# First batch of a two-part kernel: first cast ahead of the inducing points, denominators from the summed exps, idle products in the waits

## The chip, the cores and the metric

The kernel runs on one core of a Trainium2 chip. The metric is device microseconds of that core for one execution. Every execution also lists its span (first to last instruction in the profiler's clock) and the mean granted clock of TensorE over it.

## The reference

```
def mab(q, kv):                       # scale = 1/sqrt(128)
    a = softmax(scale * q @ kv.T);  return a @ kv
h   = mab(I, x)                       # I: 32 inducing points, x: 4 x 12416 x 128
y   = mab(x, h).reshape(49664, 128)
g, v = y @ w_gate, y @ w_val          # 128 x 1536 each
out = y + sigmoid(y @ w_res) * ((gelu(g) * v) @ w_out)
```

A batch has 12416 tokens, 97 blocks of 128, loaded as 13 tiles of up to 8 blocks. h of a batch must be complete before the second attention of that batch can start. For batches 2 to 4 that is done behind the work of the batch before; for the first batch nothing is there to hide it. The change edits only this start.

## The kernel before

PE multiplies, ACT takes exps and gelus and copies, DVE multiplies gelu by value and casts, POOL adds and casts. The loading of the first batch, with cuts marked:

```
wb = bank_f()
for i in range(WARM):                          # 9 products on zeros, ahead of all else
    pe.matmul(wb, warm[:, :P], warm[:, :TOK], start=True, stop=True)
i1t_ps = bank_g()
pe.transpose(i1t_ps[:, :M], ind_f, ident[:M, :M])     # inducing points
ve.tensor_copy(I1T, i1t_ps[:, :M])
...
convert_hi(0, 0, ve)                           # cast of tile 0
for n in range(ntile + 2):
    if n + 1 < ntile:
        convert_hi(0, n + 1, act if n == 0 else ve)
    if n < ntile:
        turn_pe(0, n, act if n < 10 and n % 2 == 0 or n == ntile - 1 else ve)
    if 1 <= n <= ntile:
        exps("a", 0, n0, n0 + w, bank_v())     # n0, w of tile n - 1
        if n < ntile - 1:
            add_up(n0, w)                      # POOL: s += e
        if n == ntile - 1:
            weight_cast(2, act)
    if n >= 2:
        ...                                    # total(): column sums of s and the last e into acc
        accumulate(0, n0, n0 + w, n == 2, n == ntile + 1)     # sums of h, tile n - 2
```

`total` put the denominators of the softmax into a 129th column of the accumulator (ones as moving operand, s as stationary one). After the last sum all 129 columns were copied (nacc in the profile); `turn_first_h` turned the denominators by one more product, inverted them (zi) and scaled the turned h (ht):

```
pe.matmul(tp[:, 0:M], na[:, P:P + 1].to_broadcast([P, P]), strips[:, 0, :], ...)
pe.matmul(tp[:, P:2 * P], na[:, 0:P], row, ...)
ve.reciprocal(zi, tp[:, 0:M])
ve.tensor_tensor(ht, tp[:, P:2 * P], zi, AL.mult)             # shapes cut
```

Then come the exps of the second attention, the first layer with h folded into the weights, a table load on ACT and the first gelus. From there a fixed order of products, gelus and multiplications runs to the end.

The softmax here doesn't subtract the row's maximum and nothing guards it: scores larger than these inputs give would overflow.

Of the kernel before, what the change touches and what calls it, by code (L numbers as in the profile page):

```python
# [9 lines left out]
FP32 = mybir.dt.float32  # L10
# [4 lines left out]
AL = mybir.AluOpType  # L15
# [3 lines left out]
def kernel(  # L19
# [25 lines left out]
    P = 128  # L45
# [3 lines left out]
    FCH = F // P  # L49
    nblk = N // P  # L50
    PRE = 8
    WARM = 9
    ntile = (nblk + PRE - 1) // PRE
    Q = 4
    scale = 1.0 / math.sqrt(C)
# [26 lines left out]
    def bank_g():  # L82
        return ps_g.tile([P, TOK], FP32, name="g", tag="g")

    def bank_v():
        return ps_v.tile([P, 2 * TOK], FP32, name="v", tag="v")

    def bank_f():
        return ps_f.tile([P, TOK], FP32, name="f", tag="f")
# [4 lines left out]
    def blocks_of(k):  # L94
        return k * PRE, min(PRE, nblk - k * PRE)
# [20 lines left out]
    def convert_hi(b, k, eng):  # L116
        _, w = blocks_of(k)
        hi_t[b, k] = hi = sized(p_hl, w, P, "hi")
        if eng is act:
            act.activation(hi[:, :w, :], xf_t[b, k][:, :w, :], AC.Copy, bias=0.0, scale=1.0)  # L120
        else:
            eng.tensor_copy(hi[:, :w, :], xf_t[b, k][:, :w, :])  # L122
# [15 lines left out]
    def turn_pe(b, k, eng=act):  # L138
        _, w = blocks_of(k)
        xt = sized(p_xt, w, P, "xt")  # L140
        xt_t[b, k] = xt
        tps = bank_g().bitcast(FP16).rearrange("p (k c) -> p k c", c=P)
        for j in range(w):
            pe.transpose(tps[:, j, :], hi_t[b, k][:, j, :], identF)  # L144
        if eng is act:
            act.activation(xt[:, :w, :], tps[:, :w, :], AC.Copy, bias=0.0, scale=1.0)
        else:
            eng.tensor_copy(xt[:, :w, :], tps[:, :w, :])
# [28 lines left out]
    def accumulate(b, j0, j1, first, last):  # L177
        if first:
            acc_t[b] = bank_f() if b == 0 else bank_g()
        acc = acc_t[b]  # L180
        for j in range(j0, j1):
            k, jj = divmod(j, PRE)
            cq = j % Q
            o = acc[cq * M:(cq + 1) * M, :]
            e = e_of.pop(("a", b, j))
            if b == 0:
                pe.matmul(o[:, 0:P], e, xf_t[b, k][:, jj, :],  # L187
                          start=(first and j < j0 + Q), stop=(last and j + Q >= j1),
                          skip_group_check=True)
                continue  # L190
            pe.matmul(o[:, 0:P + 1], e, lo_t[b, k][:, jj, :P + 1],
                      start=(first and j < j0 + Q), stop=False, skip_group_check=True)
            pe.matmul(o[:, 0:P], e, hi_t[b, k][:, jj, :],
                      start=False, stop=(last and j + Q >= j1), skip_group_check=True)
        if last:
            if b not in nacc_t:
                nacc_t[b] = p_h.tile([P, P + 1], FP32, name="nacc", tag="nacc", bufs=1)
                ve.tensor_copy(nacc_t[b], acc[:, :P + 1])
            else:
                na = nacc_t[b]  # L200
                ve.tensor_tensor(na, acc[:, :P + 1], na, AL.add)
            del acc_t[b]

    def add_up(n0, w):

        e = e_t["a", n0 // WIDE * WIDE][:, n0 % WIDE * M:(n0 % WIDE + w) * M]
        if "s" not in e_of:
            e_of["s"] = p_sm.tile([P, PRE * Q * M], FP16, name="a2", tag="a2").bitcast(FP32)[:, :w * M]
            po.tensor_copy(e_of["s"], e)
        else:  # L210
            po.tensor_tensor(e_of["s"], e_of["s"], e, AL.add)

    def total(s):

        n = s.shape[1]
        for q in range(0, n, Q * M):
            r = min(Q * M, n - q)
            pe.matmul(acc_t[0][:r, P:P + 1], s[:, q:q + r], one,
                      start=False, stop=False, skip_group_check=True)

    def finish_h(b, hs=None):
        if hs is None:
            hs = bank_g()
            pe.matmul(hs[:, 0:P + 1], strips.rearrange("p q m -> p (q m)"), nacc_t.pop(b),
                      start=True, stop=True)
        rz = p_h.tile([P, 1], FP32, name="rz1", tag="rz1")
        ve.reciprocal(rz, hs[:, P:P + 1])
        hf = p_h.tile([P, P + 1], FP32, name="nacc", tag="nacc", bufs=1)[:, :P]
        ve.tensor_scalar(hf, hs[:, 0:P], rz, None, op0=AL.mult)
        hf_t[b] = hf  # L230

        hra = p_h.tile([P, 2, P], FP16, name="hra", tag="hra")
        hra_t[b] = hra
        po.memset(hra[2 * M:, 0, :], 0.0)
        po.memset(hra[:2 * M, 1, :], 0.0)
        po.tensor_copy(hra[2 * M:, 1, :], hf[2 * M:, :])
        po.tensor_tensor(hra[3 * M:, 1, :], hf[3 * M:, :], hra[3 * M:, 1, :], AL.subtract)

        if b not in hgv_t:
            hgv_t[b] = p_h.tile([P, F], BF16, name="hgv", tag="hgv")  # L240

    def turn_first_h(b):

        na = nacc_t[b]
        tp = bank_g()
        row = strips.rearrange("p q m -> p (q m)")
        pe.matmul(tp[:, 0:M], na[:, P:P + 1].to_broadcast([P, P]), strips[:, 0, :],
                  start=True, stop=True)
        pe.matmul(tp[:, P:2 * P], na[:, 0:P], row, start=True, stop=True)
        zi = p_h.tile([P, M], FP32, name="zi", tag="zi", bufs=1)  # L250
        ve.reciprocal(zi, tp[:, 0:M])
        ht = p_h.tile([P, P], FP16, name="ht", tag="ht")
        ve.tensor_tensor(ht.rearrange("p (q m) -> p q m", m=M),
                         tp[:, P:2 * P].rearrange("p (q m) -> p q m", m=M),
                         zi.unsqueeze(1).to_broadcast([P, Q, M]), AL.mult)
        ht_t[b] = ht
        hgv_t[b] = p_h.tile([P, F], BF16, name="hgv", tag="hgv")
# [12 lines left out]
    def first_layer_out(b, c, bank):  # L270
        ve.tensor_scalar(hgv_t[b][:, c:c + TOK], bank, parts, None, op0=AL.mult)
# [243 lines left out]
    ve.tensor_tensor(strips[:, 0, :], strips[:, 0, :], ident[:, 3 * M:4 * M], AL.add)  # L515
    for q in range(1, Q):
        ve.tensor_copy(strips[:, q, :], strips[:, 0, :])
    wb = bank_f()
    for i in range(WARM):
        pe.matmul(wb, warm[:, :P], warm[:, :TOK], start=True, stop=True)  # L520
    i1t_ps = bank_g()
    pe.transpose(i1t_ps[:, :M], ind_f, ident[:M, :M])
    ve.tensor_copy(I1T, i1t_ps[:, :M])

    pieces = []
    for dst, src, o, w in ((wG, moe_w_gate, 0, TOK), (wV, moe_w_val, 0, TOK),
                           (wG, moe_w_gate, TOK, 2 * TOK), (wV, moe_w_val, TOK, 2 * TOK),
# [15 lines left out]
    def weight_cast(i, eng):  # L543
        dst, src, w = pieces[i]
        if eng is act:
            act.activation(dst, staged.pop(i)[:, :w], AC.Copy, bias=0.0, scale=1.0)
        else:
            eng.tensor_copy(dst, staged.pop(i)[:, :w])
# [2 lines left out]
    for i in range(len(pieces)):  # L551
        weight_in(i)

    tiles = list(range(ntile))
    convert_hi(0, 0, ve)
    for n in range(ntile + 2):
        if n + 1 < ntile:
            convert_hi(0, n + 1, act if n == 0 else ve)
        if n < ntile:
            turn_pe(0, n, act if n < 10 and n % 2 == 0 or n == ntile - 1 else ve)  # L560
        if 1 <= n <= ntile:
            n0, w = blocks_of(n - 1)
            exps("a", 0, n0, n0 + w, bank_v())
            if n < ntile - 1:
                add_up(n0, w)
            if n == ntile - 1:
                weight_cast(2, act)
        if n >= 2:
            n0, w = blocks_of(n - 2)
            if n == ntile:  # L570
                total(e_of.pop("s"))
                total(e_t["a", n0 // WIDE * WIDE][:, n0 % WIDE * M:(n0 % WIDE + w) * M])
            if n == ntile + 1:
                total(e_t["a", n0 // WIDE * WIDE][:, :w * M])
            accumulate(0, n0, n0 + w, n == 2, n == ntile + 1)
    weight_cast(0, po)
    weight_cast(1, po)
    weight_cast(3, act)
    weight_cast(4, po)
    turn_first_h(0)  # L580
    half = PRE // 2
    exps("b", 0, 0, half, bank_g())
    sums_b(0, 0, half, ve)
# [4 lines left out]
    sums_b(0, half, WIDE, po)  # L588
    layers = bank_v()
    first_layer(0, 0, layers[:, :TOK])  # L590
    first_layer(0, TOK, layers[:, TOK:])
    first_layer_out(0, 0, layers[:, :TOK])
    exps("b", 0, WIDE, 2 * WIDE, bank_v())
    turned()
    later = [(j0, min(j0 + WIDE // 2, nblk)) for j0 in range(2 * WIDE, nblk, WIDE // 2)]
    for j in later:
        exps("b", 0, *j, bank_g())
    first_layer_out(0, TOK, layers[:, TOK:])
    weight_cast(5, po)
    ones_b(0, half, WIDE)  # L600
# [8 lines left out]
    def rest_of_first():  # L609
        layers = bank_v()  # L610
        first_layer(0, 2 * TOK, layers[:, :TOK])
        rs, hs = layers[:, TOK:TOK + P], layers[:, TOK + P:TOK + 2 * P + 1]
        pe.matmul(rs[:64, :], ht_t[0][:, :64], wR, start=True, stop=True)
        pe.matmul(hs, strips.rearrange("p q m -> p (q m)"), nacc_t.pop(0), start=True, stop=True)
        first_layer_out(0, 2 * TOK, layers[:, :TOK])
        finish_h(0, hs)
        res_layer(0, ve, rs)
# [249 lines left out]
```

## Time and profile before

| view of the kernel before | value |
|---|---|
| time of the first three runs, median | 773.27 us (772.80 to 773.37) |
| profiled execution | 771.35 us, span 769.6, clock 0.989 |
| busy PE, ACT, DVE | 97%, 97%, 96% of the span |
| half clock within the first 50 us | 3.41 + 3.41 + 10.23 us |
| first product on DVE | 37.23 us |

How to read it: with three engines at 96 to 97% over 769.6 us, what is left to win is where the digits of the clock row and of the first slices are below 9. The lines themselves are shown in the prediction.

### The profile page before, as it was taken

Reading aid. Unit: us, or ns where it says so; the run is one execution under the profiler, and the core shown is the slowest. Engines: PE = TensorE matmul, PEld = TensorE weight load, DVE = VectorE, ACT = ScalarE, POOL = GpSimd, SP = SyncE. Lnnn points to the kernel's source line nnn. Section 1 sums busy time; section 2 is a strip of 40 time slices with the busy share of each in tenths; the row PEclk is TensorE's granted clock in tenths of the full one; section 3 lists DMA queues with packets and bytes.
Section 4 is the critical chain, followed back from the end, with each engine's and each line's share of the span. In section 5 each row is a group of like instructions: output and inputs, shape, how many; then the busy total and the mean of one; then the engine's idle time right before and its main releaser. Section 6 shows DMA issues by size and latency. Waiting matters only on the chain.

```text
span 769.6 us, 23941 instructions
## 1 busy us (share of the span) xinstructions
PE 744.0 (97%) x9602; PEld 433.1 (56%) x9602; DVE 736.1 (96%) x737; ACT 744.0 (97%) x1494; POOL 470.4 (61%) x464
## 2 busy tenths in 40 slices
PE   8899999999999999999999999999999999999997
PEld 5545456565655555565655555566565545555654
DVE  5599999999999999989999999999999999999997
ACT  4699999999999999999999999999999999999997
POOL 3636998711777979723377788852267664543444
PEclk9889999999999999999999999999999999999999
DMA  9314598601164487510044567850006341101111
GB/s 344 124 43 121 142 214 181 150 29 43 43 114 103 119 202 199 152 42 29 30 90 101 113 164 171 201 117 30 34 25 130 73 99 43 43 29 43 42 43 47
DMA packets 118449, 78.16 MB, mean 102 GB/s; under 512 B 96672, under 2 KB 99392, under 8 KB 118336
## 3 DMA queue, kind: packets, MB, share of 16 engines
q1 hardware_dynamic: 118336, 76.62, 39.5%
q8 instruction: 75, 1.23, 0.7%
q14 instruction: 38, 0.31, 0.1%
HBM read 27.87 MB, written 25.43 MB: 69 GB/s over the span
## 4 chain that ended last, share of the span: by engine, by line
PE 48%; ACT 34%; issue 10%; DVE 5%; POOL 2%; DMA 1%; DVEq 0%; SPq 0%; ACTq 0%; POOLq 0%
ACT ge L419 25%; PE f L442 21%; PE g L408 11%; PE v L408 7%; DVE u L413 5%; PE g L450 3%; ACT th L456 3%; ACT at L461 3%; ACT fe L470 1%; ACT e L172 1%; PE g L169 1%; PE f L187 1%; PE g L144 1%; DVE th L474 1%; POOL lo L128 1%
## 5 line engine op out<-in xcount | busy, mean ns | idle before, releaser
L413 DVE TENSOR_TENSOR u<-ge,v 128x1024 bf16<-128x1024 f32 x584 | 670.8, 1212 | 6.2 <-PE v L408 1.2
L419 ACT ACTIVATE ge<-g 128x512 f32<-128x512 f32 x1164 | 605.2, 658 | 2.9 <-PE g L408 2.6
L442 PEld LDWEIGHTS <-u 128*128 128x128 bf16 x4656 | 270.3, 98 | 214.3 <-issue 209.7
L442 PE MATMUL f<-wO,u 128*128 128x128 bf16 x4656 | 374.2, 221 | 4.2 <-DVE th L474 0.9
L408 PE MATMUL g<-rt,hgv 32*128 32x512 f16 x1152 | 336.9, 381 | 7.8 <-ACT ge L419 0.5
L408 PE MATMUL v<-rt,hgv 32*128 32x512 f16 x1152 | 222.7, 386 | 1.9 <-DVE u L413 1.3
L475 POOL TENSOR_TENSOR at<-at,th 128x512 f32<-128x512 f32 (+1 forms) x99 | 123.7, 1250 | 131.4 <-ACT ge L419 40.0
L408 PEld LDWEIGHTS <-hgv 32*128 32x128 bf16 x2400 | 74.3, 91 | 87.7 <-issue 21.7
L471 POOL TENSOR_TENSOR th<-th,fe 128x512 f32<-128x512 f32 (+1 forms) x33 | 39.7, 1202 | 96.3 <-ACT fe L470 96.3
L343 POOL TENSOR_TENSOR a<-e,z 128x1024 f16<-128x1024 f32 (+1 forms) x48 | 89.8, 1880 | 8.7 <-DMA rt<-a 4.7
L128 POOL TENSOR_TENSOR lo<-xf,hi 128x1024 f16<-128x1024 f32 x36 | 76.9, 2137 | 0.2
L450 PE MATMUL g<-hra,rt 128*128 128x128 f16 x768 | 71.3, 219 | 1.3
L461 ACT ACTIVATE at<-g 128x512 f32<-128x512 f32 (+1 forms) x100 | 63.7, 647 | 0.1
L456 ACT ACTIVATE th<-g 128x512 f32<-128x512 f32 (+1 forms) x100 | 63.4, 646 | 0.2
L450 PEld LDWEIGHTS <-rt 128*128 128x128 f16 x768 | 50.6, 97 | 9.6 <-issue 7.7
L474 DVE SCALAR_TENSOR_TENSOR th<-th,f 128x512 f32<-128x512 f32 (+1 forms) x67 | 45.4, 678 | 3.3 <-PE f L442 1.5
L122 POOL CAST hi<-xf 128x1024 f16<-128x1024 f32 x36 | 37.3, 1037 | 14.4 <-DMA xf<-in_x_dram 12.4
L472 POOL TENSOR_TENSOR at<-at,fe 128x512 f32<-128x512 f32 (+1 forms) x33 | 39.7, 1203 | 0.0
L319 POOL TENSOR_TENSOR a<-e 128x512 f32<-128x512 f32 (+1 forms) x12 | 15.3, 1278 | 22.4 <-ACT e L172 22.4
L169 PEld LDWEIGHTS <-xt 128*128 128x128 f16 x768 | 23.7, 97 | 5.0 <-issue 3.8
L172 ACT ACTIVATE e<-g 128x512 f32<-128x512 f32 (+3 forms) x40 | 20.9, 602 | 2.3 <-PE g L169 2.3
L322 POOL TENSOR_TENSOR a<-a 128x256 f32<-128x256 f32 (+8 forms) x48 | 20.1, 418 | 3.8
(136 smaller groups left out, 259.7 us busy)
## 6 DMA issues: line engine op xcount, KB each, us to landing
out_dram<-at SPq DMA_DIRECT2D x96, 256.0 KB, 2.3
xf<-in_x_dram SPq DMA_DIRECT2D x39, 512.0 KB, 4.4
ge<-in_x_dram SPq DMA_DIRECT2D x9, 512.0 KB, 7.6
rt<-a SPq DMA_TRANSPOSE x48, 3.1
xt<-hi SPq DMA_TRANSPOSE x36, 4.3
ge<-in_moe_w_gate_dram SPq DMA_DIRECT2D x1, 512.0 KB, 8.3
ge<-in_moe_w_val_dram SPq DMA_DIRECT2D x1, 512.0 KB, 7.9
ge<-in_moe_w_out_dram SPq DMA_DIRECT2D x1, 512.0 KB, 7.3
```

Source lines behind the costliest of these rows:

```text
L128: eng.tensor_tensor(lo[:, :w, :P], xf_t.pop((b, k))[:, :w, :], hi_t[b, k][:, :w, :], AL.subtract)
L343: eng.tensor_tensor(a2[:, :n], ev[:, o:o + n, :].unsqueeze(2).to_broadcast([P, n, Q, M]), z[:, o:o + n].unsqueeze(2).unsqueeze(3).to_broad ...
L408: pe.matmul(*t[n], start=True, stop=True)
L413: ve.tensor_tensor(u[:, :n], ge_t.pop(value)[:, :n], v_t.pop(value)[:, :n], AL.mult)
L419: act.activation(ge_t[i][:, h * TOK:h * TOK + n], gb[:, :n], AC.Gelu, bias=0.0, scale=1.0)
L442: pe.matmul(self.ffn[:, k, :], u_t[self.gi, si][:, o:o + P], wO[:, fc, :], start=first, stop=not self.todo, skip_group_check=True)
L450: pe.matmul(bank[:, k * P:(k + 1) * P], rt_t[self.b, self.k][:, self.j0 + k, :], hra_t[self.b][:, s, :], start=True, stop=True)
L456: act.activation(self.th[:, :self.tw], self.mix(0), AC.Tanh, bias=0.0, scale=0.5)
L461: act.activation(self.at[:, :self.tw], self.mix(1), AC.Copy, bias=0.0, scale=1.0)
L471: po.tensor_tensor(th, th, fe, AL.mult)
L474: ve.scalar_tensor_tensor(th, th, 1.0, f, AL.add, AL.mult)
L475: (ve if self.gi == ngrp - 1 else po).tensor_tensor(at, at, th, AL.add)
```

## The change

The intent is to bring the first products forward and to keep TensorE's clock up meanwhile. An idle product is a product on zeros whose result is never read; it only keeps PE busy. Core of the diff (helpers cut):

```diff
-        ve.tensor_copy(nacc_t[b], acc[:, :P + 1])
+        n = P + (b > 0)
+        ve.tensor_copy(nacc_t[b][:, :n], acc[:, :n])
-    def total(s):                       # column sums into acc[:, P:P + 1]
+    def total(zb):
+        s = e_of.pop("s")
+        for k in (ntile - 2, ntile - 1):
+            ...
+            ve.tensor_tensor(s[:, :w * M], s[:, :w * M], e, AL.add)
+        n = s.shape[1] // M
+        for j in range(n):
+            pe.matmul(zb, one.to_broadcast([P, P]), s[:, j * M:(j + 1) * M],
+                      start=(j == 0), stop=(j == n - 1))
+    def idle(n, bank=None):
+        ...                             # n products 128x512 on zeros, never read
-    i1t_ps = bank_g()                   # moved behind the first turned tile
...
     convert_hi(0, 0, ve)
-    for n in range(ntile + 2):
...
+    for n in range(ntile - 1):
+        convert_hi(0, n + 1, ve)
+        turn_pe(0, n, act if n < 10 and n % 2 == 0 else ve)
+        if n == 0:
+            ...                         # inducing points
+            idle(2)
+        if n == ntile - 2:
+            turn_pe(0, n + 1, act)
+        if n >= 1:
+            step_e(n - 1)
+        if n == 1:
+            idle(2)
+        if n >= 2:
+            step_s(n - 2)
+    weight_cast(2, act)
+    step_e(ntile - 2)
+    step_e(ntile - 1)
+    step_s(ntile - 3)
+    zb = bank_g()[:, :M]
+    step_s(ntile - 2)
+    total(zb)
+    step_s(ntile - 1)
+    idle(1, bank_g())
...
-    turn_first_h(0)
+    turn_first_h(0, zb)                 # reciprocal straight from zb
+    idle(3)
...
     first_layer(0, 0, layers[:, :TOK])
-    first_layer(0, TOK, layers[:, TOK:])
...                                      # all other exps of the second attention
+    first_layer(0, TOK, layers[:, TOK:])
     first_layer_out(0, TOK, layers[:, TOK:])
...
-        pe.matmul(hs, strips..., nacc_t.pop(0), start=True, stop=True)
+        pe.matmul(hs[:, :P], strips..., nacc_t.pop(0)[:, :P], start=True, stop=True)
+        zi = e_of.pop("zi")
+        for q in range(Q):
+            pe.matmul(hs[q * M:(q + 1) * M, P:P + 1], zi, ident[:, 0:1], ...)
+        idle(5)
```

More of the change, by code (lines that the diff above doesn't have):

```diff
@@ L51 @@
     PRE = 8
-    WARM = 9
     ntile = (nblk + PRE - 1) // PRE
@@ L211, in add_up @@
             po.tensor_tensor(e_of["s"], e_of["s"], e, AL.add)
-    def total(s):
-        n = s.shape[1]
-        for q in range(0, n, Q * M):
-            r = min(Q * M, n - q)
-            pe.matmul(acc_t[0][:r, P:P + 1], s[:, q:q + r], one,
-                      start=False, stop=False, skip_group_check=True)
+    def total(zb):
+        s = e_of.pop("s")
+        for k in (ntile - 2, ntile - 1):
+            n0, w = blocks_of(k)
+            e = e_t["a", n0 // WIDE * WIDE][:, n0 % WIDE * M:(n0 % WIDE + w) * M]
+            ve.tensor_tensor(s[:, :w * M], s[:, :w * M], e, AL.add)
[4 more added lines that the diff above has]
+    def idle(n, bank=None):
+        bank = bank_f() if bank is None else bank
+        for i in range(n):
+            pe.matmul(bank, warm[:, :P], warm[:, :TOK], start=True, stop=True)
     def finish_h(b, hs=None):
@@ L226, in finish_h @@
         rz = p_h.tile([P, 1], FP32, name="rz1", tag="rz1")
-        ve.reciprocal(rz, hs[:, P:P + 1])
+        if b == 0:
+            ve.tensor_copy(rz, hs[:, P:P + 1])
+        else:
+            ve.reciprocal(rz, hs[:, P:P + 1])
         hf = p_h.tile([P, P + 1], FP32, name="nacc", tag="nacc", bufs=1)[:, :P]
@@ L240, in finish_h, with turn_first_h @@
             hgv_t[b] = p_h.tile([P, F], BF16, name="hgv", tag="hgv")
-    def turn_first_h(b):
+    def turn_first_h(b, zb):
         na = nacc_t[b]
-        tp = bank_g()
-        row = strips.rearrange("p q m -> p (q m)")
-        pe.matmul(tp[:, 0:M], na[:, P:P + 1].to_broadcast([P, P]), strips[:, 0, :],
-                  start=True, stop=True)
-        pe.matmul(tp[:, P:2 * P], na[:, 0:P], row, start=True, stop=True)
-        zi = p_h.tile([P, M], FP32, name="zi", tag="zi", bufs=1)
-        ve.reciprocal(zi, tp[:, 0:M])
+        tp = bank_g()[:, :P]
+        pe.matmul(tp, na[:, 0:P], strips.rearrange("p q m -> p (q m)"), start=True, stop=True)
+        zi = e_of["zi"] = p_h.tile([P, M], FP32, name="zi", tag="zi", bufs=1)
+        ve.reciprocal(zi, zb)
         ht = p_h.tile([P, P], FP16, name="ht", tag="ht")
         ve.tensor_tensor(ht.rearrange("p (q m) -> p q m", m=M),
-                         tp[:, P:2 * P].rearrange("p (q m) -> p q m", m=M),
+                         tp.rearrange("p (q m) -> p q m", m=M),
                          zi.unsqueeze(1).to_broadcast([P, Q, M]), AL.mult)
@@ L517 @@
         ve.tensor_copy(strips[:, q, :], strips[:, 0, :])
-    wb = bank_f()
-    for i in range(WARM):
-        pe.matmul(wb, warm[:, :P], warm[:, :TOK], start=True, stop=True)
-    i1t_ps = bank_g()
-    pe.transpose(i1t_ps[:, :M], ind_f, ident[:M, :M])
-    ve.tensor_copy(I1T, i1t_ps[:, :M])
+    idle(9)
     pieces = []
@@ L552, with step_e, step_s @@
         weight_in(i)
-    tiles = list(range(ntile))
-    convert_hi(0, 0, ve)
-    for n in range(ntile + 2):
-        if n + 1 < ntile:
-            convert_hi(0, n + 1, act if n == 0 else ve)
-        if n < ntile:
-            turn_pe(0, n, act if n < 10 and n % 2 == 0 or n == ntile - 1 else ve)
-        if 1 <= n <= ntile:
-            n0, w = blocks_of(n - 1)
-            exps("a", 0, n0, n0 + w, bank_v())
-            if n < ntile - 1:
-                add_up(n0, w)
-            if n == ntile - 1:
-                weight_cast(2, act)
-        if n >= 2:
-            n0, w = blocks_of(n - 2)
-            if n == ntile:
-                total(e_of.pop("s"))
-                total(e_t["a", n0 // WIDE * WIDE][:, n0 % WIDE * M:(n0 % WIDE + w) * M])
-            if n == ntile + 1:
-                total(e_t["a", n0 // WIDE * WIDE][:, :w * M])
-            accumulate(0, n0, n0 + w, n == 2, n == ntile + 1)
+    def step_e(n):
+        n0, w = blocks_of(n)
+        exps("a", 0, n0, n0 + w, bank_v())
+        if n < ntile - 2:
+            add_up(n0, w)
+    def step_s(n):
+        n0, w = blocks_of(n)
+        accumulate(0, n0, n0 + w, n == 0, n == ntile - 1)
+    convert_hi(0, 0, ve)
+    for n in range(ntile - 1):
+        convert_hi(0, n + 1, ve)
+        turn_pe(0, n, act if n < 10 and n % 2 == 0 else ve)
+        if n == 0:
+            i1t_ps = bank_g()
+            pe.transpose(i1t_ps[:, :M], ind_f, ident[:M, :M])
+            ve.tensor_copy(I1T, i1t_ps[:, :M])
+            idle(2)
[5 more added lines that the diff above has]
+            idle(2)
+        if n >= 2:
+            step_s(n - 2)
[8 more added lines that the diff above has]
+    idle(1, bank_g())
     weight_cast(0, po)
@@ L613, in rest_of_first @@
         pe.matmul(rs[:64, :], ht_t[0][:, :64], wR, start=True, stop=True)
-        pe.matmul(hs, strips.rearrange("p q m -> p (q m)"), nacc_t.pop(0), start=True, stop=True)
+        pe.matmul(hs[:, :P], strips.rearrange("p q m -> p (q m)"), nacc_t.pop(0)[:, :P],
+                  start=True, stop=True)
+        zi = e_of.pop("zi")
+        for q in range(Q):
+            pe.matmul(hs[q * M:(q + 1) * M, P:P + 1], zi, ident[:, 0:1], start=True, stop=True)
+        idle(5)
         first_layer_out(0, 2 * TOK, layers[:, :TOK])
```

## The prediction

> **What bounds the kernel now.** I read the page first. Its busy line has three engines at 96 to 97% of a 769.6 us span:
>
> ```profile
> PE 744.0 (97%) x9602; PEld 433.1 (56%) x9602; DVE 736.1 (96%) x737; ACT 744.0 (97%) x1494; POOL 470.4 (61%) x464
> ...
> PEclk9889999999999999999999999999999999999999
> ```
>
> The reader should see that nothing is left in the middle, and that the TensorE clock is below full only in slices 2 and 3 (19 to 58 us). The change edits only the first batch's start, which ends there. So everything turns on when the steady stream of gelu (ACT), product (DVE) and matmul (PE) begins, and at what clock. A microsecond won there moves the end by about a microsecond, because the order of instructions after it is fixed and full.
>
> Next I read the busy times in windows whose edges are the steps of the clock (columns: stretch, length, then busy of PE, PEld, DVE, ACT, POOL, then clock, DMA share, GB/s):
>
> ```profile
> 5.12:8.54 3.42, 1.38 (x18) 1.03 (x17) 1.25 (x3) 1.74 (x2) 0.00 (x0) 1.00 0.91 341
> 8.54:11.95 3.41, 3.02 (x46) 2.57 (x47) 2.23 (x4) 2.02 (x4) 0.80 (x2) 0.50 1.03 419
> 11.95:22.19 10.24, 10.24 (x252) 8.37 (x250) 8.06 (x12) 5.81 (x11) 7.36 (x8) 1.00 1.03 402
> 22.19:25.60 3.41, 2.87 (x69) 2.06 (x61) 1.08 (x3) 1.38 (x5) 2.80 (x5) 1.00 1.03 290
> 25.60:29.02 3.42, 2.29 (x31) 1.84 (x31) 0.94 (x3) 1.57 (x3) 0.30 (x1) 1.00 0.09 21
> 29.02:32.43 3.41, 3.38 (x78) 2.53 (x78) 1.91 (x4) 1.59 (x4) 1.51 (x2) 0.50 0.02 5
> 32.43:35.85 3.42, 2.81 (x44) 1.55 (x41) 1.78 (x4) 3.39 (x7) 3.19 (x7) 1.00 0.00 0
> 35.85:46.08 10.23, 9.45 (x59) 3.72 (x58) 9.36 (x12) 8.61 (x17) 3.59 (x7) 0.50 0.20 39
> ```
>
> Three half-clock stretches, 3.41, 3.41 and 10.23 us, each after a window in which PE was lightly used. In the last one ACT is idle 10.23 - 8.61 = 1.62 us and DVE 10.23 - 9.36 = 0.87 us; the list of groups of that stretch puts 1.5 and 0.8 us of it down to waiting for PE's gate products. Before 25 us the DMA share is 1.03: the loading of x is bound by transfers.
>
> Last, the chain of waits between the last x tiles and the first product:
>
> ```profile
> 23.45 0.54 issue
> ...
> 25.47 0.88 PE f L218 x8
> 26.35 0.56 PE f L187 x14
> ...
> 27.22 0.30 DVE nacc L198
> ...
> 27.57 0.41 PE g L247 x2
> ...
> 28.32 0.37 DVE zi L251
> ...
> 28.71 0.30 DVE ht L253
> ...
> 29.05 0.59 PE g L169 x16
> ...
> 30.07 0.99 PE v L268 x2
> ...
> 37.23 1.23 DVE u L413
> ```
>
> It shows what the change is about: the softmax denominator is summed by PE inside the accumulation (L218), turned and inverted after it (L247, L251), and only then can the second set of exps start (29.05).
>
> **What the Trainium skill says.** "TensorE: Matmul & The Clock Gate", Part 1, What's actually happening: the clock is half or full, set by how busy PE was in a free-running window of 3413 ns. The trace agrees: only 0.50 and 1.00, in steps of 3.41 us. But its rule of no PE idle gap over about 3 us is too weak here: no gap before 29.02 was over 0.8 us, and the clock fell. Same page, LDWEIGHTS (loading the stationary operand): time goes with the columns, columns / 1.2 ns, 107 ns for 128. The chain agrees: 8 passes of L218 in 0.88 us are 0.11 us each; a fp32 product is two passes in this trace (8 products of L187 stand as x16, 0.57 us, 0.036 each, with 32 columns). Same page, Architectural detail: ACT and DVE are strict FIFO. "DMA: Bandwidth & Descriptors", Queues, rings and completion order: each DMA engine takes descriptors in ring order. Consistent here: x tiles land in the order of issue, and issuing earlier into a full queue should not make them land earlier.
>
> **The change, part by part.**
>
> (1) First cast ahead of the inducing points, on DVE. Tile 0 lands about 3.7 us after its issue at 0.75 (the shortest landing of that group), at 4.5; its cast now starts at 6.45, behind the inducing points that land at 1.67 + 4.29 = 5.96. It will start near 4.6, and the first transposes near 5.3 in place of 7.19. But the next tiles come by DMA: DVE waits 0.95 us for tile 2 until 8.08, waits again for tiles 4, 8 and 10, and its casts run in order ahead of the copies. Transposes of tile 11 need its landing (11.46 + 9.7 = 21.1) plus a cast of 0.69: 21.9, against 22.35 now. So of 1.9 us won at the front at most 0.4 reaches the last tile. The idle products (2 + 2) should also keep full clock in 8.54 to 11.95, hidden by the same transfers.
>
> (2) Denominator. Out of the accumulation go the L218 products (0.88 + 0.03 us), and out of the chain L247 (0.41) and the reciprocal from it (0.37), which now runs beside the remaining product; against that nacc to ht should take 0.30 + 0.04 + 0.47 + 0.03 = 0.84 instead of 28.71 - 27.22 = 1.49: 0.65 won. In go two short DVE adds (hidden beside the accumulation) and 8 fp32 products with the ones as stationary operand: 16 passes of 0.11 = 1.76 us, in PE's order before the last block's sum, so on the path. Against 0.91 removed that is 0.85 lost. Net 0.2 lost.
>
> (3) A moved cast. The 128x1024 weight cast on ACT (1.05 us) now stands ahead of the exps of tile 11, not behind them. Its weights land 8.3 us after their issue at 15.70, at 24.0, whatever happens on PE. ACT being FIFO, these exps start at 24.0 + 1.05 = 25.05; now 24.81. The exps of the last block come sooner (about 25.4 for 26.03), because they no longer stand behind the cast. Carrying on: exps end 25.43, sum of tile 11 to 26.05, denominators to 27.8, last block 28.07, ht done about 28.9 and ht itself 0.3 more, 29.2, against 29.0. The 0.4 us of (1) is lost in this wait, and so is the 0.54 us issue gap at 23.45 if it vanishes.
>
> (4) Idle products behind turn_first_h: 3 x 0.216 = 0.65 us at full clock. They start about 28.7 and end about 29.4, while ht comes at 29.2: 0.15 us lost.
>
> (5) The second pair of first-layer products moves behind the exps, into PE's 0.41 us wait for a bank: 0.49 us (half of the 0.99 row) leaves the path, and another 0.25 if the remaining pair runs at full clock.
>
> (6) Late idle products (5, 1.08 us): PE waited there for ACT's table and gelus, 0.50 us before the row at 36.26, and the first product is set by DVE's chain (37.23). Four short fp32 products for 1/denominator add about 0.3 us ahead of that chain. Hidden or small.
>
> Sum to the first product: the second set of exps starts at 29.4 in place of 29.05 (steps 1 to 4 together), +0.35; step 5 takes off 0.5 to 0.75, step 6 adds about 0.1: about -0.2 us, within +-0.4.
>
> (7) The clock. If the window before 35.85 holds its clock by the five idle products, the 10.23 us of half clock vanish. ACT then loses little of its 1.5 us of waits for gates, DVE little of 0.8. I take 1.2.
>
> Together -0.2 - 1.2 = -1.4 us if the clock holds to the end of the start; I give that 65%. If it does not, idle products at half clock cost 0.43 us each where they stand on the path: about +0.3. The mean is 0.65 x -1.4 + 0.35 x 0.3 = -0.8; since the counts (9, 2, 2, 1, 3, 5) look tuned to the waits, I go a little further: -1.3 us, 772.0 for 773.27.
>
> **Rivals.** (a) The DMA bound gives way less than thought, in the good direction: if what delays x is not total transfer but the order of buffers, the 1.9 us at the front survives and the time is near 770. Against it: a DMA share of 1.03 from 8.54 to 22.19. (b) The moved cast as new wait: PE is idle from about 24.3 to 25.4 because ACT waits for weights; this empties the window 22.19 to 25.60 and brings half clock at 25.6, right where denominators and h are formed. Then those take up to 1 us longer, and the total is 773 to 773.8. For it: PE's busy share there falls from 84% to about 65%. Against it: weight loads did not slow at half clock (32 exps' products took 0.98 us then), and the denominators are bound by these. (c) Nothing reaches the end: the schedule behind 50 us has its own waits, and the later batches are untouched. ACT 97% with 100% in 46 to 56 us speaks for passing gains on.
>
> **Range and chances.** The clock outcome and run spread (772.8 to 773.37 before) give 770.2 to 773.5 for 8 in 10. 2% is 15.5 us, nearly half of the whole start: faster 0.01, same 0.985, slower 0.005.
>
> **What would show it right or wrong.** Casts of x: tile 0 near 4.6 us, tile 11 still near 21.1 to 21.8 (if 19 to 20, step 1 is wrong). ACT: the 128x1024 cast starts on a DMA wait near 24, exps of tile 11 near 25.0. PE: the 8 denominator products take about 1.8 us; if 1 us, ht comes 0.7 earlier. ht done near 29.2, first product near 36.9. Clock: 1.00 from 32 us on. A half-clock stretch after 35 us would take away most of the gain; a first product before 35.5 us, or a gain over 3 us, would mean that I have the transfers or the path through the denominators wrong.

## The result, and the profile after

| | before | changed |
|---|---|---|
| median, first measurement (4 runs each) | 773.32 us | 772.00 us |
| median, repeated with 5 rounds (11 and 6 runs) | 772.40 us | 771.75 us |
| ratio, first measurement | | 0.9979 (0.9961 to 0.9997) |
| ratio, repeated | | 0.9992 (0.9978 to 1.0006) |

A ratio is the mean time of one kernel's runs over that of the other's of the same rounds, so it is not quite the ratio of the medians beside it. The predicted time of 772.0 was met; the gain is 1.3 us by the first medians (1.6 by the means), but 0.65 in the repetition, where the interval takes in 1. The total being right says nothing yet about its terms, and they were not all right.

The profiled execution of the changed kernel is a warning. It took 772.73 us, 1.4 more than the profiled one of before, though the medians say the opposite. From its page, busy time and clock:

```profile
PE 745.3 (97%) x9627; PEld 434.4 (56%) x9627; DVE 736.9 (96%) x740; ACT 742.7 (96%) x1493; POOL 469.5 (61%) x464
...
PEclk9899999999999999999999999999999999999999
```

The low digit has moved from slices 2 and 3 to slice 2 alone. The windows of its start, cut at the steps of the clock (columns as in the prediction):

```profile
3.92:7.33 3.41, 2.69 (x32) 1.63 (x30) 1.49 (x3) 1.02 (x1) 0.00 (x0) 1.00 0.91 312
7.33:24.40 17.07, 14.55 (x326) 11.11 (x323) 11.81 (x18) 8.13 (x17) 8.60 (x11) 1.00 1.04 396
24.40:27.81 3.41, 2.52 (x52) 1.96 (x50) 0.94 (x2) 2.32 (x4) 2.27 (x4) 1.00 0.46 118
27.81:34.63 6.82, 6.70 (x68) 4.57 (x68) 2.20 (x7) 1.28 (x3) 0.38 (x1) 0.50 0.00 0
34.63:44.87 10.24, 8.73 (x117) 4.29 (x114) 7.86 (x13) 9.29 (x18) 7.92 (x13) 1.00 0.12 24
```

There is one half-clock stretch of 6.82 us where before had 3.41 + 10.23, not counting the early 3.41. But it lies on the worst place: ACT is busy 1.28 us in it. Its chain of waits (start, length, what; rows left out at the dots):

```profile
24.33 1.06 ACT wG L550
...
25.77 0.76 DVE a L219
...
26.62 0.20 DVE a L219
...
26.86 2.79 PE g L222 x16
29.66 0.57 PE f L186 x2
...
30.77 0.64 PE g L259 x2
31.41 1.28 PE f L229 x3
...
40.60 0.48 DVE u L423
```

The eight products for the denominators (two passes each, x16) take 2.79 us. In the records of the single passes, they start every 0.112 us up to 27.78 and every 0.214 us from 27.98 on: the drop of the clock falls in their middle. The three idle products after them (L229, 1.28 us) now hold up the exps, and the first product comes at 40.60 us against 37.23. Comparing the k-th DVE product of both profiles, the changed kernel is 3.37 us late at the first, 1.74 at the ninth, and 1.42 from the 31st to nearly the end: two of the three lost microseconds come back between 37 and 53 us, where before runs at half clock and the changed kernel does not (that this is the cause is shown below). The shift then stays (1.38 at the last product), as the prediction had assumed of a full schedule.

Front of the changed kernel, DVE in order of time:

```profile
4.41 0.69 DVE L121 CAST hi<-ge 128x1024 f16<-128x1024 f32 x1 [1.90 <-DMA ge<-in_x_dram]
...
8.45 0.69 DVE L121 CAST hi<-ge 128x1024 f16<-128x1024 f32 x1 [1.96 <-DMA ge<-in_x_dram]
```

The cast of tile 0 starts at 4.41, but the third tile's still waits 1.96 us for its transfer.

### The profile page after: what moved, and what is told of

Its sections match the earlier page's. It is cut to its first block, busy times and chain, and to the rows that moved or that the text cites. A ratio compares the mean times of both kernels' runs of the same rounds, so it can differ in the third digit from the quotient of the medians.

```text
span 771.0 us, 23999 instructions
## 1 busy us (share of the span) xinstructions
PE 745.3 (97%) x9627; PEld 434.4 (56%) x9627; DVE 736.9 (96%) x740; ACT 742.7 (96%) x1493; POOL 469.5 (61%) x464
## 4 chain that ended last, share of the span: by engine, by line
PE 45%; ACT 35%; issue 10%; DVE 6%; DMA 2%; POOL 1%; SPq 0%; DVEq 0%; ACTq 0%; POOLq 0%
ACT ge L429 25%; PE f L452 20%; PE g L418 11%; PE v L418 7%; DVE u L423 5%; ACT th L466 3%; ACT at L471 3%; PE g L460 3%; ACT e L171 1%; ACT fe L480 1%; DMA ge<-in_moe_w_gate_dram 1%; PE g L168 1%; DMA ge<-in_x_dram 1%; POOL lo L127 1%; ACT L171 1%
```

## The experiments

Theories: A, the time is set by how much of the start runs at half clock, and where; the idle products are the part of the change that wins. B, the chain of instructions sets the time and the clock is a by-product. Later ones, C and D, are named where they were written. All kernels gave correct results. The table at the end has all the numbers.

### Both kernels once more

No edit, to see the spread: the granted clock differs from execution to execution.

> The kernel before, unchanged, to see the spread of its clock. The profiled execution of before took 771.35 us with 13.65 us of half clock between 8.5 and 46.1, yet its unprofiled runs took 772.8 to 774.6. Theory A (time follows how much of the start runs at half clock, which depends on where the free-running 3.41 us windows fall): times spread over 1 to 3 us and the mean clock of each run falls as its time rises; ratio to before 1.000 +- 0.0015. Theory B (the chain of instructions alone sets the time): times within 0.5 us, no relation to the clock.

> The changed kernel, unchanged. Theory A: again 770.8 to 772.8, with the runs at clock 0.998 fastest and those at 0.994 slowest; its profile has at most two half-clock windows after 8 us. If the profile falls on another phase than the first one (half clock 27.8 to 34.6), the first product comes 1 to 3 us before the 40.6 us seen there. Theory B: first product again at 40.6 +- 0.3 us whatever the clock.

Measured: before again 772.60 us, ratio 1.0006 (0.9991 to 1.0021), clock 0.983 to 0.990; changed again 771.75 us, clock 0.992 to 0.999. Over 39 executions of before that list their clock, the median is 773.5 for the 18 below 0.9865 and 772.2 for the 21 from 0.987 up. For the changed kernel (10 executions) 771.0 for the two from 0.996 up and 772.1 for the eight below. So one and the same program differs by over 1 us with the clock: A holds within a kernel. Half-clock time, (1 - clock) x 770 / 0.5, is on average 20.5 us for before and 7.9 for the changed kernel; a straight line through the 39 points gives 0.16 us of time for each microsecond of half clock, so this difference is worth about 2 us (an estimate; the correlation is 0.70, and 7.9 lies outside the 14 to 29 us of these points).

The changed kernel's second profile kept full clock until 40.57, then had one stretch at half:

```profile
40.57:47.39 6.82, 6.46 (x54) 3.68 (x50) 6.50 (x6) 5.91 (x12) 0.00 (x0) 0.50 0.22 43
```

So it shows the same path as above at full clock (timeline: start, length, engine, line, operation, tile, idle before; rows left out at the dots):

```profile
24.59 0.36 ACT L171 ACTIVATE e<-v 128x256 f32<-128x256 f32 x1
24.86 0.19 ACT L171 ACTIVATE es<-v 128x32 f32<-128x32 f32 x1
...
25.07 0.59 DVE L219 TENSOR_TENSOR a<-a,e 128x256 f32<-128x256 f32 x1 [1.60 <-ACT es L171]
25.77 0.19 DVE L219 TENSOR_TENSOR a<-a,es 128x32 f32<-128x32 f32 x1
...
26.01 1.97 PE L222 MATMUL g<-a,one 128*128 128x32 f32 x16 [0.35 <-DVE a L219]
...
27.91 0.41 PE L186 MATMUL f<-u,es 128*32 128x128 f32 x2
...
28.36 0.29 DVE L198 COPY nacc<-f 128x128 f32<-128x128 f32 x1 [2.40 <-PE f L186]
...
29.23 0.29 DVE L263 TENSOR_TENSOR ht<-g,zi 128x128 f16<-128x128 f32 x1 [0.32 <-PE g L259]
```

From the end of the exps of tile 11 (24.95) to the end of ht (29.52) it takes 4.57 us; in before 25.19 to 29.00, 3.81. The new path is 0.76 us longer even at full clock. The first product came at 37.67, 3 us earlier than in the first profile: B, which expected 40.6 again, is out.

### The weight cast put back

```diff
-    weight_cast(2, act)
     step_e(ntile - 2)
     step_e(ntile - 1)
+    weight_cast(2, act)
```

> The changed kernel with the 128x1024 weight cast on ACT put back behind the exps of the last two tiles. If the moved cast holds up the denominators (step 3 of the prediction), the exps of tile 11 end near 24.7 in place of 25.65, the denominator products start 0.7 to 1.0 us earlier (near 26.0), PE's idle window before them shrinks, and the time falls by 0.5 to 1.5 us below the changed kernel's, below 771.3. If the wait is hidden (the last block or the cast itself is needed as early by the first layer), the time stays within 0.4 us of the changed kernel's.

Measured: 771.60 us, ratio 0.9984 (0.9971 to 0.9997), against 0.9992 of the changed kernel in the same rounds: the intervals overlap, so no cost of the cast is shown. In the profile the exps of tile 11 ran at 24.71, the denominators at 26.35: neither sooner than in the profile just shown. PE had a gap there for which the profile names nothing ("issue", 0.7 us at most in this run's list of waits), and the exps' products came late for another reason than the cast.

This profile is worth more for something else. It kept full clock from 5.8 us to 767. The same stretch that in before stood at half clock:

```profile
35.85:46.08 10.23, 9.00 (x91) 4.20 (x90) 9.72 (x13) 9.97 (x22) 4.50 (x7) 1.00 0.22 42
```

ACT is busy 9.97 us, not 8.61, with 22 instructions, not 17. From the first product to the 41st it takes 48.90 us, in before 50.85: full clock in this stretch alone is worth 1.95 us. The kernel's first product was 0.77 us later than before's, and its 41st 1.18 us earlier. The other profiles settle that this is the clock and not the new order. With full clock there, the 41 products took 48.90 us in three profiles of the new order (this one, the changed kernel's first, one product) and 49.10 in one of the old order (before with idle products and two more). With the 10.24 us stretch they took 50.86 and 50.87 in the new order (the next two experiments). And the 6.82 us at half clock in the changed kernel's second profile cost nearly as much: 50.50.

### Without the idle products

```diff
-            idle(2)        # behind the inducing points
-            idle(2)        # n == 1
-    idle(1, bank_g())
-    idle(3)
-        idle(5)            # the first nine stay
```

> The changed kernel with all idle products taken out but the nine at the very start. If the idle products pay by holding the clock, half-clock windows come back after 35 us (and at 8 to 12), mean clock 0.988 to 0.990, and the time rises by 1 to 2 us over the changed kernel's, to that of before or above. If they only stand in the way, or the clock is set by the useful work, the time stays or falls by up to 0.5 us.

Measured: 773.28 us, ratio 1.0007 (0.9993 to 1.0021), clock 0.983 to 0.990. Both half-clock stretches are back, at 31.07 (3.42 us) and 37.90 (10.24 us), and so is the early one at 10.59. Without them the rest of the change wins nothing.

### The five late idle products alone taken out

```diff
-        idle(5)
```

> The changed kernel without the five idle products among the rest of the first batch, the others kept. If these five are what keeps the clock after 35 us, the profile has 3.4 to 10.2 us of half clock between 33 and 48 us, mean clock at 0.986 to 0.991, time as of before (0.999 to 1.001). If the earlier ones do it, the clock stays at 0.993 to 0.999 and the time at the changed kernel's or 0.3 us below.

Measured: 773.04 us, ratio 0.9996 (0.9979 to 1.0012), clock 0.989 to 0.992. The windows of its profile:

```profile
34.79:38.21 3.42, 2.72 (x31) 1.22 (x28) 1.64 (x3) 3.39 (x8) 3.19 (x7) 1.00 0.00 0
38.21:48.45 10.24, 9.66 (x61) 3.83 (x61) 9.45 (x12) 8.23 (x16) 3.53 (x6) 0.50 0.21 42
```

Without these five, 1.1 us of multiplying zeros, the 10.24 us stretch is back, and no execution has a clock above 0.992, the changed kernel's lowest. In time the two cannot be told apart (0.9996 here, 0.9992 there, in other rounds).

### The idle products alone, in the kernel before

```diff
     ve.tensor_copy(I1T, i1t_ps[:, :M])
+    idle(2)
...
             exps("a", 0, n0, n0 + w, bank_v())
+            if n == 1:
+                idle(2)
...
+    idle(1, bank_g())
...
     turn_first_h(0)
+    idle(3)
...
+        idle(5)
         first_layer_out(0, 2 * TOK, layers[:, :TOK])
```

> The kernel before with nothing changed but the idle products, in the same waits (2 and 2 in the loading, 1 and 3 around the turning of h, 5 among the rest of the first batch). Theory C (the whole gain is the clock that the idle products hold; the rest of the change only lengthens the chain to the first product by 0.3 to 1 us): mean clock 0.993 to 0.999, time 1.2 to 2.2 us below that of before (ratio 0.9970 to 0.9985), at or below the changed kernel's. Theory D (clock and the shortened chain belong together; idle products in the old waits stand on its longer chain): ratio 0.999 to 1.001.

Measured: 769.93 us, ratio 0.9961 (0.9943 to 0.9979). Theory D is out, and theory C holds in kind but was too low: this alone wins 3 us, where C expected 1.2 to 2.2, and more than the whole change. Its runs fall in two groups, four at clock 0.999 (769.2 to 770.3 us) and two at 0.994 and 0.995 (771.6 and 772.0).

### One product for the denominators

```diff
-        n = s.shape[1] // M
-        for j in range(n):
-            pe.matmul(zb, one.to_broadcast([P, P]), s[:, j * M:(j + 1) * M], ...)
+        sr = p_h.tile([P, M], FP32, name="sr", tag="sr", bufs=1)
+        ve.reduce_sum(sr, s.rearrange("p (j m) -> p m j", m=M), axis=AX)
+        pe.matmul(zb, one.to_broadcast([P, P]), sr, start=True, stop=True)
```

> The changed kernel with the eight fp32 products for the denominators (1.79 us at full clock, 2.79 us where half the clock fell among them) replaced by one DVE sum over the eight blocks and one product (two passes). If these products are on the path, the denominators end 0.8 to 1.4 us sooner after the exps, the first product starts near 36.5 in a profile at full clock, and the time falls 0.7 to 1.5 us below the changed kernel's, ratio 0.9965 to 0.998. If something else ends there (the last block's sum, weights, the table load of ACT), within 0.3 us of it.

Measured: 770.35 us, ratio 0.9958 (0.9940 to 0.9976). The median is 1.4 us below the changed kernel's of the rounds before, at nearly the same clocks (0.994 to 0.999, there 0.992 to 0.999); by the ratios to before, each in its own rounds, it is 2.6. The path shows 0.75 of it. From the end of the last block's exps to the end of ht it takes 3.72 us, against 4.47 at full clock and 5.99 in the changed kernel's first profile. The first product at 37.85 missed the 36.5 expected: the clock dropped for 3.41 us at 28.80 in this profile. In the profile of the last version below, at full clock, it came at 36.65.

### Both repairs, and two more idle products

The cast put back and one product:

> Both repairs: one product for the denominators, and the weight cast behind the exps of the last tiles. If the two costs add, 0.2 to 0.6 us below one_product; in the profile the exps of tile 11 do not wait for the cast. If the cast then holds up the first layer or the casts of the weights after it, the same time as one_product.

Measured: 770.07 us, ratio 0.9958 (0.9942 to 0.9975), the same as with one product alone. Again no cost of the moved cast. The next adds two idle products where PE waits for the first DVE product:

```diff
+            if i == 1:
+                idle(2)
             for f in windows.pop(i, []):
```

> The changed kernel with one product for the denominators, the cast late, and the same two more idle products. Candidate for the best version: if the two hold the clock, all runs at 0.997 or more and a median of 769.3, ratio to before 0.995; if not, 770.0 as without them.

Measured: 769.33 us, ratio 0.9953 (0.9940 to 0.9967), all five runs at clock 0.996 or more. This is the fastest median of all, 2.4 us below the changed kernel's (other rounds; 0.9953 and 0.9992 as ratios). Its path to ht at full clock:

```profile
25.68 0.19 DVE L219 TENSOR_TENSOR a<-a,es 128x32 f32<-128x32 f32 x1
25.91 0.60 DVE L221 TENSOR_REDUCE sr<-a 128x32 f32<-128x256 f32 x1
...
26.56 0.41 PE L222 MATMUL g<-sr,one 128*128 128x32 f32 x2 [1.18 <-DVE sr L221]
...
27.34 0.29 DVE L198 COPY nacc<-f 128x128 f32<-128x128 f32 x1 [0.84 <-PE f L186]
```

DVE's sum of 0.60 us and two passes stand where sixteen took 1.97. The same two idle products in the kernel before:

> The kernel before with the idle products and two more behind the second slot's products, where PE waits 0.3 to 0.5 us for the first DVE product. The runs with idle products fall into two groups, clock 0.999 at 769.2 to 770.3 us and 0.994 at 771.6 to 772.0. If the window before the drop was just too light, more runs keep 0.999 and the median falls to 769.5; if it does not help, the same two groups and 769.9 to 770.5.

Measured: 770.54 us, ratio 0.9968 (0.9952 to 0.9985), again four runs at 0.998 or more and two below: they did not help there. So whether they are what kept the clock in the version above is not shown; five runs without a drop can be luck.

### Two parts of the change on top of the idle products

Tile 0's cast first, as the change has it (the inducing points behind the first turned tile, the second cast on DVE):

> The kernel before with the idle products and with part 1 of the change alone: tile 0 cast on DVE and turned ahead of the inducing points, the second tile's cast on DVE too. Prediction, step 1: the front is won (cast of tile 0 at 4.4 in place of 5.7 or 6.5), but tile 11 still waits for its transfer, so at most 0.4 us reaches the end: ratio to before 0.9950 to 0.9965, where the idle products alone gave 0.9961. If the front survives (rival a): 1 us or more, ratio under 0.995.

Measured: 770.21 us, ratio 0.9968 (0.9953 to 0.9983). The cast of tile 0 starts at 4.38, tile 11 lands at 20.4 and is turned at 21.90. With the idle products alone these are 20.1 and 21.93. Nothing of the front reaches tile 11 in these profiles, and the ratio is no better.

The second pair of first-layer products moved:

> The kernel before with the idle products and with part 5 alone: the second pair of first-layer products behind the exps. Prediction, step 5: 0.5 to 0.75 us off the path from ht to the first gelu, which is 6.1 to 6.5 us in the profiles of before and of before with idle products: 5.6 or less, ratio to before 0.9950 to 0.9955. If ACT's own exps and table load set that stretch, as the changed kernel's 6.25 us suggest: unchanged, 6.0 to 6.4 us, ratio 0.996.

Measured: 771.11 us, ratio 0.9974 (0.9957 to 0.9991). From the end of ht to the first ACT instruction after the table load it takes 6.14 us with it and 6.14 without, in both profiles at full clock (in the second but for its last 0.4 us). Their chains of waits, with the pair moved and then with the idle products alone:

```profile
30.80 1.23 ACT e L172 x3
...
36.52 0.20 ACT gel L618
```

```profile
29.88 1.23 ACT e L172 x3
...
33.15 0.58 ACT e L172
...
35.69 2.13 PE f L225 x5
...
38.48 0.40 DVE u L419
```

The step into the chain is ACT's exps (L172) 0.4 us after ht, and the pair is in neither chain. The second chain shows something else: in this profile of before with idle products the clock fell at 35.22, the five late idle products (L225) took 2.13 us, and the first product came 2.87 us after the ACT instruction behind the table load, 1.71 in the other.

### All runs

| kernel | us, median | ratio to before (95%) | clock |
|---|---|---|---|
| before, again | 772.60 | 1.0006 (0.9991 to 1.0021) | 0.983 to 0.990 |
| changed, again | 771.75 | 0.9992 (0.9978 to 1.0006) | 0.992 to 0.999 |
| cast late | 771.60 | 0.9984 (0.9971 to 0.9997) | 0.994 to 0.999 |
| no idle | 773.28 | 1.0007 (0.9993 to 1.0021) | 0.983 to 0.990 |
| no late idle | 773.04 | 0.9996 (0.9979 to 1.0012) | 0.989 to 0.992 |
| before + idle | 769.93 | 0.9961 (0.9943 to 0.9979) | 0.994 to 0.999 |
| before + idle + cast first | 770.21 | 0.9968 (0.9953 to 0.9983) | 0.994 to 0.997 |
| before + idle + pair moved | 771.11 | 0.9974 (0.9957 to 0.9991) | 0.992 to 0.999 |
| before + idle + 2 more | 770.54 | 0.9968 (0.9952 to 0.9985) | 0.994 to 0.999 |
| one product | 770.35 | 0.9958 (0.9940 to 0.9976) | 0.994 to 0.999 |
| one product, cast late | 770.07 | 0.9958 (0.9942 to 0.9975) | 0.994 to 0.999 |
| one product, cast late, 2 more idle | 769.33 | 0.9953 (0.9940 to 0.9967) | 0.996 to 1.000 |

## Why the prediction was right, and where it was not

The time, 772.0, was right, and so was its frame: a shift made in the first 50 us stays to the end (rival (c) is out, though of the 2.40 us by which the last version leads at its 41st product 2.03 are left at the last), and the clock is the larger of the two terms. All ten executions lie in its range. That 772.0 was hit so closely is luck: the working gave a gain of 0.8 us and was moved to 1.3 because the counts of idle products looked tuned, and both terms behind it were off. The first product was to come 0.2 us sooner than before's 37.23. In the second profile, at full clock, it came 0.44 us later (0.68 counted from the end of the exps of tile 11: 12.72 us, in before 12.04), in the first 3.37. The clock was to win 1.2 us and wins 1.95 where the stretch of the first 41 products is free of half clock, but most executions still had a drop. The errors nearly cancelled.

1. **First cast.** Right. The cast started at 4.41, and that of tile 11 at 21.60 in the changed kernel's first profile; alone, the part changed nothing (0.9968 with it, 0.9961 without). Rival (a) is out: the third tile's cast waits 1.96 us for its transfer.

2. **Denominators.** The products were sized right at full clock (1.97 us with their start and end, for 1.76) and so was the way from nacc to the start of ht (28.36 to 29.23, 0.87 for 0.84). What failed is that the two DVE adds were called hidden. They start only when the last exps are done and end 1.0 us after the exps of tile 11; PE waits 0.35 us for them, 0.51 in the first profile. With the last block's sum that makes the path 0.76 us longer than before's. The replacement by one product makes that path 0.75 us shorter again; its gain in time, about 1.4 us on the medians, has a part that no path here accounts for.

3. **Moved cast.** Its times were right (it starts at 24.33 upon its transfer, the exps of tile 11 follow it on ACT at 25.29, in order as cited), its cost is not shown: putting it back gave 0.9984 for 0.9992, and with one product 0.9958 for 0.9958.

4. **Three idle products.** Right at full clock: ht ends at 29.52 and the exps' products start at 29.68, 0.16 us later for 0.15. At half clock it was 0.75 us (31.73 to 32.48).

5. **Second pair of first-layer products.** Wrong. I took 0.5 to 0.75 us off the path because the pair stood in before's chain of waits. It stood there at half clock. At full clock the chain runs through ACT's exps, and the pair moved or not, it is 6.14 us.

6. **Late idle products and the four short ones.** Right: from the ACT instruction behind the table load to the first product 1.71 us before, 1.90 in the changed kernel at full clock. It is 1.90 without the five late idle products too, so the 0.19 is not theirs.

7. **Clock.** The mechanism was right, the size too small: 1.2 us from the idle time of ACT and DVE in the list of waits, 1.95 measured. ACT's 1.5 us of waits in that stretch came to less than the stretch cost; where the rest was lost is not shown. "If the clock holds" was also not an either-or, and "1.00 from 32 us on" came true in neither profile of the changed kernel (half clock to 34.63 in the first, from 40.57 to 47.39 in the second). Of 10 executions 2, at 0.998 and 0.999, can have kept full clock; the 8 at 0.995 or below cannot, and even those are above all of before (0.991 at most).

Rival (b), the moved cast emptying a window so that the clock drops under the denominators, happened in the changed kernel's first profile (2.52 us of PE in 24.40 to 27.81, then 6.82 us at half clock). My argument against it, that weight loads do not slow at half clock, was wrong for these: 0.112 us a pass became 0.214. Whether the cast or the adds emptied the window is open. And no gap "over 0.8 us" before 29.02 is not quite so for the whole start: PE had one of 0.89 us, at 6.31; after 25.60 the longest is 0.77.

The sum as measured, at full clock on both sides: the new path is 1.06 us longer than the old one (from the end of the exps of tile 11 to the first product 12.72 us, against 11.66 in before with idle products and tile 0's cast first). Of this the way to ht has 0.76, the way from ht to the ACT instruction behind the table load 0.11, the rest 0.19. The times agree: changed kernel 771.0 at clock 0.996 or more (only two executions), before with idle products, in all its four variants, 769.9 there (13 executions). Against it stand about 2 us for the clock (20.5 to 7.9 us of half clock at 0.16). That leaves 0.9, between the 1.3 and 0.65 us that the two measurements gave. The direct test, in the rounds of the repetition, gives less for both, with noise of about 1 us: the changed kernel without idle products is at 1.0007, with them at 0.9992, so the rest loses 0.5 us and they win 1.2 (1.5 by the medians).

## What to carry to other kernels

Before working on a chain of waits, look at the clock of the stretch in which it lies, and compare several executions: here one program varied by over 1 us with its clock, and the two profiled executions alone would have given the wrong sign. Idle products that stand where PE waits anyway cost nothing that shows at full clock (1.90 us with the five and without), but they are on the path if the clock has fallen when they run (2.13 us for five, 1.28 for three). They are worth trying by themselves, ahead of any reordering. A row in a chain taken at half clock is not a measure of what removing it wins at full clock.

## What the Trainium skill lacked or had wrong

- "TensorE: Matmul & The Clock Gate", Why this matters for your kernels, advises no PE idle gap over about 3 us between bursts. Here the clock fell after windows in which no gap was over 0.8 us (before, 25.60 to 29.02, PE busy 2.29 of 3.42 us). So partial load of a window is enough. The same page's section on a second failure mode does tell of short idles between groups that make the clock swing; neither place says how much load is enough.
- The same page, Part 1, says that busy-ness of the window decides, but not how it is counted. PE's busy time in the profile is not it: a window with 2.69 us (changed kernel, 3.92 to 7.33, mostly products over all 128 rows) kept full clock, one with 2.81 us (before, 32.43 to 35.85, with products over 32 rows among them) lost it. That the rows make the difference was not tested.
- The same page, LDWEIGHTS (loading the stationary operand), gives columns / 1.2 ns without a word of the clock. Passes of fp32 products with 128 stationary columns came every 0.112 us at full and every 0.214 us at half clock; 16-bit ones with 128 columns and 32 moving ones came every 0.025 us at full and every 0.027 at half clock. Whether it is the load or the product that doubles in the fp32 pass is open.
- The same page (Part 1) says that the ramp is run-variable and small, under 1% of a typical kernel. Neither is contradicted here: over 39 executions of before the clock was 0.981 to 0.991, with about 1.3 us between the medians of its two halves, 0.17%. That is as much as the whole change moved.
